# A gated dilated convolution on one core: one store for the last group, and first rows turned by products instead of transposes

## The chip, the cores and the metric

The kernel runs on 1 core of one Trainium2 chip. The metric is device time in microseconds (us) of one execution; the kernel before took 285.28 us (median of three runs). The engines are named as the profile names them: PE is TensorE (PEld its weight loads), DVE is VectorE, ACT is ScalarE, POOL is GpSimd, SP is SyncE; SPq and ACTq are the queues on which SP and ACT issue transfers.

## What is computed

The input x is 2 x 16000 x 256 in bf16, w is 3 x 256 x 512, w_o is 256 x 256.

```
xp = jnp.pad(x, ((0, 0), (pad, 0), (0, 0)))        # pad = 4, dilation 2
h = jnp.einsum('btc,cd->btd', xp[:, pad:pad + T, :], w[0])
for i in range(1, K):                               # K = 3
    off = pad - i * dil
    h = h + jnp.einsum('btc,cd->btd', xp[:, off:off + T, :], w[i])
f, g = h[..., :D], h[..., D:]
z = jnp.tanh(f) * _sigmoid(g)
return z @ w_o
```

Each output row needs its own row of x and those two and four rows before it.

## The kernel before

**Layout.** Four successive rows of x make one "r"; T / 4 = 4000 of them per batch are cut into groups of at most 256 (`groups`, built at lines 60 to 73). The first group of batch 0 has 160, the last two of batch 1 have 128 each. A tile `xt` holds a chunk of x turned, with channels on the partitions: `xt[:, j, ct, r]`, j being the row within the four. Rows j = 0, 1 are the x half, j = 2, 3 the y half; `views` (line 157) gives current and previous r of both as xc, yc, xp, yp.

**Steady work.** Groups 1 and on compute two rows per bank from sums and differences: DVE and POOL prepare `m`, `p` and `d` (lines 163 to 191), PE runs eight 128x512 products per step k (`products`, line 193, one step per group and block of 128 output channels), ACT copies bank b (`copy_m2`, line 234), DVE adds and subtracts in PSUM (`combine`, line 241), ACT applies tanh and sigmoid (`activate`, line 249), DVE multiplies (`gate`, line 266), and PE multiplies by w_o (`out_mm`, line 289). `out_evict` (line 303) copies the result to an SBUF tile `osb` and SP stores it. The order of all instructions is written by hand (`tc.manual_schedule()`, loop at lines 398 to 439). A group of 160 leaves 32 rows over: these "odd rows" are gated into `zo` and stored by four transfers of 32 partitions each (lines 308 to 314).

**The start.** At line 112 DVE clears a 128x128 tile `warm`, and PE multiplies it by itself 30 times (`warm_up(N_WARM[0])`, line 126) while the first transfers run. SP loads the first 640 rows of x as they are into `xn` (line 119); ACT issues the weights of taps 2 and 0, SP those of tap 1. Later chunks of x come by transposing transfers (line 106), which are slower to land, so the first group is turned on PE: `turn(i)` (lines 140 to 155) transposes tile i of 80 r's with the identity, 2 halves of j by 4 transposes, into a bf16 PSUM tile. The half h = 0 (rows j = 0, 1) is copied to `xt` by DVE, the half h = 1 by ACT. `turn(0)` and `turn(1)` are followed by six more warm-up products (line 370). Then the first group goes by plain products (`direct`, line 214): for each tap in the order 2, 0, 1 and each of three output blocks k, two products into bank a and two into bank b, 128x320 each. For tap 2 bank a reads only the half j = 0, 1 and bank b only the half j = 2, 3. PE then runs on with the steady steps.

**The end.** `finish` (line 324) multiplies the last group (128 r's) by w_o into four PSUM tiles (lines 340 to 347). For jp = 1 and then 0, ACT copies one tile and DVE the other into a tile `osb_end` (lines 350 and 351), and SP stores it by a transfer of 128 KB (line 353): two transfers.

Of the kernel before, what the change touches and what calls it, by code (L numbers as in the profile page):

```python
# [13 lines left out]
def kernel(  # L14
# [19 lines left out]
    nc = tc.nc  # L34
    bf16 = mybir.dt.bfloat16
    f32 = mybir.dt.float32
    B, T, D = x.shape
    K, _, D2 = w.shape
    P = 128
    assert K == 3 and D % P == 0 and D2 == 2 * D and T % 64 == 0  # L40
    CT = D // P
    NT = D // P
    RH = 16
    RG = 256
    N_WARM = (30, 6)
    O_ORDER = (0, 2, 1, 3)
    TAPS = (2, 0, 1)
    FIRST = (160,)
# [12 lines left out]
    for b in range(B):  # L61
        r0 = 0
        rs = sizes(FIRST if b == 0 else (), LAST[min(b, 1)])
        cuts = [1, 1] if b == 0 else []
        i = 0
# [10 lines left out]
    consts = ctx.enter_context(tc.tile_pool(name="consts", bufs=1))  # L76
# [7 lines left out]
    osb_pool = ctx.enter_context(tc.tile_pool(name="osb", bufs=4))  # L84
    ps_a = ctx.enter_context(tc.tile_pool(name="ps_a", bufs=3, space=bass.MemoryType.PSUM))
    ps_b = ctx.enter_context(tc.tile_pool(name="ps_b", bufs=3, space=bass.MemoryType.PSUM))
    ps_o = ctx.enter_context(tc.tile_pool(name="ps_o", bufs=2, space=bass.MemoryType.PSUM))
    ctx.enter_context(tc.manual_schedule())

    def warm_up(n):  # L90
        wps = ps_a.tile([P, 2 * RG], f32, name="a")
        for _ in range(n):
            nc.tensor.matmul(wps[:, :P], lhsT=warm[:], rhs=warm[:], start=True, stop=True)  # L93

    xts = {}

    def load_chunk(c):
# [11 lines left out]
        )  # L109


    warm = consts.tile([P, P], bf16)
    nc.vector.memset(warm[:], 0.0)  # L113
    w_taps = [consts.tile([P, CT, D2], bf16, name=f"w{k}_sb") for k in range(K)]
    wo_sb = consts.tile([P, NT, D], bf16)
    nx, rx = len(TILES), TILES[0][1]
    xn = consts.tile([P, nx, 4, D], bf16, name="xn")
    w_in = [w[k].rearrange("(ct c) d -> c ct d", c=P) for k in range(K)]
    nc.sync.dma_start(
        out=xn[:rx], in_=x[0, 0:4 * nx * rx, :].rearrange("(i r j) c -> r i j c", i=nx, j=4)  # L120
# [3 lines left out]
    nc.scalar.preload_act_table(ACT.Sigmoid)  # L124
    nc.sync.dma_start(out=w_taps[TAPS[2]][:], in_=w_in[TAPS[2]])
    warm_up(N_WARM[0])
    ident = consts.tile([P, P], bf16)
    make_identity(nc, ident[:])
# [8 lines left out]
    wp_sb = consts.tile([P, CT, D2], bf16)  # L137
    wm_sb = consts.tile([P, CT, D2], bf16)

    def turn(i):  # L140
        r0, r = TILES[i]
        for h in range(2):
            pool, tag = ((ps_o, "o_ps"), (ps_b, "b"))[i]
            tp = pool.tile([P, 2, CT, P], bf16, name="tp", tag=tag)
            for j in range(2):
                for ct in range(CT):
                    nc.tensor.transpose(  # L147
                        out=tp[:, j, ct, :r], in_=xn[:r, i, 2 * h + j, ct * P:(ct + 1) * P],
                        identity=ident[:r, :r],
                    )  # L150
            dst = xts[0][:, 2 * h:2 * h + 2, :, RH + r0:RH + r0 + r]
            if h == 0:
                nc.vector.tensor_copy(out=dst, in_=tp[:, :, :, :r])
            else:
                nc.scalar.copy(out=dst, in_=tp[:, :, :, :r])

    def views(g):
        G = groups[g]
        xt, c, R = xts[G["chunk"]], RH + G["col"], G["R"]
        return (xt[:, 0:2, :, c - 1:c - 1 + R], xt[:, 2:4, :, c - 1:c - 1 + R],  # L160
                xt[:, 0:2, :, c:c + R], xt[:, 2:4, :, c:c + R])
# [49 lines left out]
                start=first and ct == 0, stop=ct == CT - 1, skip_group_check=True,  # L211
            )

    def direct(k, taps):

        g, oi = divmod(k, 4)
        G = groups[g]
        o = O_ORDER[oi]
        osl = slice(o * P, (o + 1) * P)
        R = G["R"]  # L220
        xp, yp, xc, yc = views(g)
        for tap in taps:
            if tap == TAPS[0]:
                G["a", oi] = ps_a.tile([P, 2 * RG], f32, name="a")
                G["b", oi] = ps_b.tile([P, 2 * RG], f32, name="b")
            for bank, mv in (("a", (xc, yp, xp)[tap]), ("b", (yc, xc, yp)[tap])):
                for ct in range(CT):
                    nc.tensor.matmul(  # L228
                        G[bank, oi][:, :2 * R], lhsT=w_taps[tap][:, ct, osl], rhs=mv[:, :, ct, :],
                        start=tap == TAPS[0] and ct == 0, stop=tap == TAPS[-1] and ct == CT - 1,  # L230
                        skip_group_check=True,
                    )
# [16 lines left out]
    def activate(k):  # L249
        g, oi = divmod(k, 4)  # L250
        G = groups[g]
        R = G["R"]
        o = O_ORDER[oi]
        if oi == 0:
            G["th"] = act_pool.tile([P, NT, 4, RG], bf16, name="th")
            G["sg"] = act_pool.tile([P, NT, 4, RG], bf16, name="sg")
            G["z"] = z_pool.tile([P, NT, 4, RG], bf16, name="zz")
        dst = G["th"][:, o] if o < NT else G["sg"][:, o - NT]
        for h, bank in ((1, "b"), (0, "a")):
            nc.scalar.activation(  # L260
                out=dst[:, 2 * h:2 * h + 2, :R],
                in_=G[bank, oi][:, :2 * R].rearrange("p (q r) -> p q r", q=2),
                func=ACT.Tanh if o < NT else ACT.Sigmoid, scale=1.0 if g == 0 else 0.5,
            )
# [38 lines left out]
    def out_evict(g, rb0, jp, on_dve):  # L303
        G = groups[g]
        o_ps = G["o", rb0, jp]
        copy = nc.vector.tensor_copy if on_dve else nc.scalar.copy
        t0 = 4 * (G["r0"] + rb0)
        if jp is None:
            osb = osb_pool.tile([P, D], bf16, name="osb_odd")
            copy(out=osb[:], in_=o_ps[:, 0, :])  # L310
            rows = out[G["b"], t0:t0 + P, :].rearrange("(r j) d -> j r d", j=4)
            for j in range(4):
                nc.sync.dma_start(out=rows[j], in_=osb[j * P // 4:(j + 1) * P // 4, :])
            return
        if jp == 0:
            G["osb", rb0] = osb_pool.tile([P, 4, D], bf16, name="osb")
        osb = G["osb", rb0]
        copy(out=osb[:, 2 * jp:2 * jp + 2, :], in_=o_ps[:])  # L318
        if jp == 1:
            nc.sync.dma_start(  # L320
                out=out[G["b"], t0:t0 + 4 * P, :].rearrange("(p j) d -> p j d", j=4), in_=osb[:]
            )

    def finish(left):

        g = NG - 1
        G = groups[g]
        R = G["R"]
        assert R <= P
        dt = NT - 1  # L330
        activate(4 * g + 3)
        for piece in left:
            out_evict(*piece, False)
        for jp in (1, 0):
            js = slice(2 * jp, 2 * jp + 2)
            nc.vector.tensor_tensor(
                out=G["z"][:, dt, js, :R], in0=G["th"][:, dt, js, :R], in1=G["sg"][:, dt, js, :R], op=ALU.mult
            )
        tiles = {}
        for d in range(NT):  # L340
            for j in (2, 3, 0, 1):
                if d == 0:
                    tiles[j] = (ps_a, ps_b)[j % 2].tile([P, 2 * RG], f32, name="ab"[j % 2])
                nc.tensor.matmul(  # L344
                    tiles[j][:R, :D], lhsT=G["z"][:, d, j, :R], rhs=wo_sb[:, d, :],
                    start=(d == 0), stop=(d == NT - 1),
                )
        for jp in (1, 0):
            osb = osb_pool.tile([P, 2, D], bf16, name="osb_end")
            nc.scalar.copy(out=osb[:R, 0, :], in_=tiles[2 * jp][:R, :D])  # L350
            nc.vector.tensor_copy(out=osb[:R, 1, :], in_=tiles[2 * jp + 1][:R, :D])  # L351
            t0 = 4 * G["r0"]
            nc.sync.dma_start(
                out=out[G["b"], t0:t0 + 4 * R, :].rearrange("(p j) d -> p j d", j=4)[:, 2 * jp:2 * jp + 2, :],
                in_=osb[:R],
            )

    def drain(g, k, behind=None):

# [5 lines left out]
    NG = len(groups)  # L365
    NB = 4 * NG
    todo, made = [], []
    turn(0)
    turn(1)
    warm_up(N_WARM[1])  # L370
    for tap in TAPS:
        for k in range(3):
            direct(k, (tap,))
    nc.scalar.mul(wd0_sb[:], w_taps[0][:], 2.0)
# [11 lines left out]
    pre_d(1, 3, nc.gpsimd, last)  # L386

    direct(3, TAPS[:-1])
    products(N_DIRECT, 2)
    products(N_DIRECT, 1)  # L390
    copy_m2(N_DIRECT)
    direct(3, TAPS[-1:])
    activate(3)
    combine(N_DIRECT)
# [3 lines left out]
    k = N_DIRECT + 1  # L398
    while k <= NB:
        g, oi = divmod(k, 4)  # L400
# [7 lines left out]
        if k < NB:  # L408
            for piece in made:
                out_evict(*piece, g == NG - 1 and oi in (0, 2))  # L410
            made = []
# [27 lines left out]
        k += 1  # L439
    assert not todo  # L440
    finish(made)


# [28 lines left out]
```

## Time and profile before

| | |
|---|---|
| runs of the kernel before | 285.22, 285.28, 287.12 us |
| the profiled execution | 285.58 us |
| its span, first to last instruction | 283.6 us |
| PE busy | 279.1 us (98% of the span) |
| ACT, DVE, POOL busy | 260.8, 240.7, 126.1 us |
| first warm-up product on PE | 0.99 us after the span's start |
| first weight product (line 228) | 6.03 us |
| last product on PE starts | 279.80 us |
| second store of `osb_end` issued | 280.73 us |

How to read it: the span is what the profiler sees between the first and the last instruction; the execution's own time is 2.0 us more. A row of the timeline gives the start, the length, the engine, the line, the operation with the tile written and the tile read, a count, and in brackets how long the engine was idle before it and what ended that. PE's records overlap, since products are pipelined: the time between the starts of two says how fast they go, not the length of one.

### The profile page before, as it was taken

To read this page: it belongs to the slowest core of one execution; us is meant where nothing else is said; L and a number is where in the kernel's file an instruction comes from. 1 tells how busy PE (TensorE), PEld (TensorE's weight loads), DVE (VectorE), ACT (ScalarE), POOL (GpSimd) and SP (SyncE) were. 2 spreads that over 40 slices of the span, in tenths; PEclk is the share of its full clock that TensorE was granted. 3 is DMA by queue.
4 is the path that set the end of the run, shared out by engine and by line. 5 is a ranking of instruction groups with operands and counts; after the bars stand their busy time and mean duration, and the time that the engine had idled before them with its cause. 6 is when DMAs were issued, how large, how long until landed. Compare 5 with 4: busy or idle time off the path is not lost.

```text
span 283.6 us, 4830 instructions
## 1 busy us (share of the span) xinstructions
PE 279.1 (98%) x1624; PEld 158.2 (56%) x1624; DVE 240.7 (85%) x404; ACT 260.8 (92%) x521; POOL 126.1 (44%) x133
## 2 busy tenths in 40 slices
PE   8999999999999999999999999999999999999994
PEld 7645555555555555555555555555555555555783
DVE  1899888888888888888888888888888888888884
ACT  3689999999999999999999999999999999999995
POOL 1145454455445544544544454455445444543430
PEclk9999999999999999999999999999999999999999
DMA  8971891470925618163282823719146061311213
GB/s 213 196 153 46 194 221 42 124 179 37 226 76 88 178 61 201 74 156 110 77 189 76 184 79 103 190 48 226 47 120 177 37 162 74 82 74 72 80 74 120
DMA packets 76055, 34.50 MB, mean 122 GB/s; under 512 B 66528, under 2 KB 68064, under 8 KB 76032
## 3 DMA queue, kind: packets, MB, share of 16 engines
q1 hardware_dynamic: 75216, 33.56, 44.8%
q10 hardware_dynamic: 816, 0.66, 0.8%
q8 instruction: 12, 0.20, 0.3%
q14 instruction: 11, 0.09, 0.1%
HBM read 1.25 MB, written 16.38 MB: 62 GB/s over the span
## 4 chain that ended last, share of the span: by engine, by line
PE 98%; DVE 0%; DVEq 0%; issue 0%
PE a L209 37%; PE b L209 37%; PE o_ps L299 19%; PE a L93 1%; PE a L228 1%; PE b L228 1%; PE tp L147 0%; PE a L344 0%; DVE osb_end L351 0%; PE b L344 0%; DVEq L467 0%; DVE warm L113 0%
## 5 line engine op out<-in xcount | busy, mean ns | idle before, releaser
L184 POOL TENSOR_TENSOR dd<-xt 128x512 bf16<-128x512 bf16 (+2 forms) x125 | 125.2, 1002 | 147.7 <-DVE zz L278 64.6
L246 DVE TENSOR_TENSOR b<-a,ss 128x512 f32<-128x512 f32 (+2 forms) x128 | 86.5, 676 | 33.6 <-ACT ss L239 32.3
L247 DVE TENSOR_TENSOR a<-a,ss 128x512 f32<-128x512 f32 (+2 forms) x128 | 85.3, 667 | 0.0
L239 ACT COPY ss<-b 128x512 f32<-128x512 f32 (+2 forms) x128 | 72.8, 569 | 12.3 <-PE b L209 0.8
L209 PEld LDWEIGHTS <-wd_sb 128*128 128x128 bf16 x512 | 50.0, 98 | 56.2 <-issue 0.7
L209 PE MATMUL a<-dd,wd_sb 128*128 128x512 bf16 (+2 forms) x256 | 73.8, 370 | 0.0
L209 PE MATMUL b<-mm,wm_sb 128*128 128x512 bf16 (+2 forms) x256 | 73.8, 370 | 0.0
L209 PE MATMUL a<-pp,wp_sb 128*128 128x512 bf16 (+2 forms) x256 | 73.8, 370 | 0.0
L209 PE MATMUL b<-dd,wd_sb 128*128 128x512 bf16 (+2 forms) x256 | 73.8, 370 | 0.0
L299 PE MATMUL o_ps<-wo_sb,zz 128*128 128x256 bf16 x488 | 73.2, 273 | 0.0
L318 ACT CAST osb<-o_ps 128x512 bf16<-128x512 f32 x121 | 71.8, 593 | 0.0
L299 PEld LDWEIGHTS <-zz 128*128 128x128 bf16 x488 | 47.7, 98 | 29.6
L278 DVE TENSOR_TENSOR zz<-th,sg 128x1024 bf16<-128x1024 bf16 (+1 forms) x65 | 42.4, 653 | 0.0
L260 ACT ACTIVATE th<-b 128x512 bf16<-128x512 f32 (+2 forms) x66 | 39.3, 595 | 2.2 <-PE b L228 1.8
L209 PEld LDWEIGHTS <-wp_sb 128*128 128x128 bf16 x256 | 25.0, 98 | 27.9
L260 ACT ACTIVATE sg<-b 128x512 bf16<-128x512 f32 (+2 forms) x66 | 39.2, 594 | 0.7 <-PE b L228 0.4
L260 ACT ACTIVATE th<-a 128x512 bf16<-128x512 f32 (+2 forms) x66 | 39.3, 596 | 0.0
L260 ACT ACTIVATE sg<-a 128x512 bf16<-128x512 f32 (+2 forms) x66 | 39.2, 595 | 0.0
L209 PEld LDWEIGHTS <-wm_sb 128*128 128x128 bf16 x256 | 25.0, 98 | 3.7
L167 DVE TENSOR_TENSOR mm<-xt 128x1024 bf16<-128x1024 bf16 (+2 forms) x32 | 21.2, 663 | 0.0
L173 DVE TENSOR_TENSOR pp<-xt 128x1024 bf16<-128x1024 bf16 (+2 forms) x32 | 21.2, 663 | 0.0
L228 PEld LDWEIGHTS <-w_sb 128*128 128x128 bf16 x48 | 4.8, 100 | 2.1
(35 smaller groups left out, 40.0 us busy)
## 6 DMA issues: line engine op xcount, KB each, us to landing
out_dram<-osb SPq DMA_DIRECT2D x61, 256.0 KB, 2.1
w_sb<-in_w_dram ACTq DMA_DIRECT2D x2, 256.0 KB, 4.6
xn<-in_x_dram SPq DMA_DIRECT2D x1, 320.0 KB, 3.6
xt<-in_x_dram SPq DMA_TRANSPOSE x17, 6.5
w_sb<-in_w_dram SPq DMA_DIRECT2D x1, 256.0 KB, 4.5
out_dram<-osb_end SPq DMA_DIRECT2D x2, 128.0 KB, 1.9
wo_sb<-in_w_o_dram ACTq DMA_DIRECT2D x1, 128.0 KB, 3.5
out_dram<-osb_odd SPq DMA_DIRECT2D x8, 16.0 KB, 1.5
```

The lines of the kernel that those rows point to most:

```text
L167: return nc.vector.tensor_tensor(out=G["m"][:, :, :, :G["R"]], in0=xc, in1=yp, op=ALU.subtract)
L173: return nc.vector.tensor_tensor(out=G["p"][:, :, :, :G["R"]], in0=xc, in1=yp, op=ALU.add)
L184: ins = eng.tensor_tensor(out=G["d"][:, j, :, :R], in0=a[:, q], in1=s[:, q], op=ALU.subtract)
L209: nc.tensor.matmul(G[bank, oi][:, :N], lhsT=wmat[:, ct, osl], rhs=mv(ct), start=first and ct == 0, stop=ct == CT - 1, skip_group_check=True,)
L228: nc.tensor.matmul(G[bank, oi][:, :2 * R], lhsT=w_taps[tap][:, ct, osl], rhs=mv[:, :, ct, :], start=tap == TAPS[0] and ct == 0, stop=tap = ...
L239: nc.scalar.copy(out=G["ss", oi][:, :N], in_=G["b", oi][:, :N])
L246: nc.vector.tensor_tensor(out=pb[:, :N], in0=pa[:, :N], in1=ss[:, :N], op=ALU.subtract)
L247: nc.vector.tensor_tensor(out=pa[:, :N], in0=pa[:, :N], in1=ss[:, :N], op=ALU.add)
L260: nc.scalar.activation(out=dst[:, 2 * h:2 * h + 2, :R], in_=G[bank, oi][:, :2 * R].rearrange("p (q r) -> p q r", q=2), func=ACT.Tanh if o ...
L278: return nc.vector.tensor_tensor(out=G["z"][:, dt, :, :full], in0=G["th"][:, dt, :, :full], in1=G["sg"][:, dt, :, :full], op=ALU.mult)
L299: nc.tensor.matmul(o_ps[:, q, :], lhsT=lhsT, rhs=wo_sb[:, dt, :], start=(dt == 0), stop=(dt == NT - 1),)
L318: copy(out=osb[:, 2 * jp:2 * jp + 2, :], in_=o_ps[:])
```

## The change

Five edits: three at the start, one at the end, one in the odd rows:

- the warm-up multiplies a one-element-per-partition constant 1.0, which the program's preamble writes anyway, read as a 128x128 operand by repeating it; the tile `warm` and DVE's memset go;
- the first rows are turned by ordinary products with the identity into an f32 PSUM tile instead of transposes into a bf16 one, with the loop turned over: half h = 0 of both tiles first, then half h = 1 of both. The half h = 0 still is DVE's to copy, h = 1 ACT's. Three warm-up products follow instead of six;
- in the first group, tap 2 is done for bank a of all three output blocks and then for bank b; taps 0 and 1 as before;
- the last group's four copies go into one `osb` tile of the pool that the other groups use (four buffers), stored by one transfer of 256 KB;
- the odd rows are stored by one transfer instead of four.

```
-    N_WARM = (30, 6)
+    N_WARM = (30, 3)
...
-            nc.tensor.matmul(wps[:, :P], lhsT=warm[:], rhs=warm[:], start=True, stop=True)
+            nc.tensor.matmul(wps[:, :P], lhsT=warm, rhs=warm, start=True, stop=True)
...
-    warm = consts.tile([P, P], bf16)
-    nc.vector.memset(warm[:], 0.0)
+    warm = nc.const_aps.tensor(1.0, (P, P), bf16)
...
-    def turn(i):
+    def turn(i, h):
         r0, r = TILES[i]
-        for h in range(2):
-            pool, tag = ((ps_o, "o_ps"), (ps_b, "b"))[i]
-            tp = pool.tile([P, 2, CT, P], bf16, name="tp", tag=tag)
-            for j in range(2):
-                for ct in range(CT):
-                    nc.tensor.transpose(
-                        out=tp[:, j, ct, :r], in_=xn[:r, i, 2 * h + j, ct * P:(ct + 1) * P],
-                        identity=ident[:r, :r],
-                    )
+        pool, tag = ((ps_o, "o_ps"), (ps_b, "b"))[h]
+        tp = pool.tile([P, 2, CT, r], f32, name="tp", tag=tag)
+        for j in range(2):
+            for ct in range(CT):
+                nc.tensor.matmul(
+                    tp[:, j, ct, :], lhsT=xn[:r, i, 2 * h + j, ct * P:(ct + 1) * P], rhs=ident[:r, :r],
+                    start=True, stop=True,
+                )
...
-    def direct(k, taps):
+    def direct(k, taps, banks="ab"):
...
-            for j in range(4):
-                nc.sync.dma_start(out=rows[j], in_=osb[j * P // 4:(j + 1) * P // 4, :])
+            nc.sync.dma_start(out=rows, in_=osb[:])
...
+        osb = osb_pool.tile([P, 4, D], bf16, name="osb")
         for jp in (1, 0):
-            osb = osb_pool.tile([P, 2, D], bf16, name="osb_end")
-            nc.scalar.copy(out=osb[:R, 0, :], in_=tiles[2 * jp][:R, :D])
-            nc.vector.tensor_copy(out=osb[:R, 1, :], in_=tiles[2 * jp + 1][:R, :D])
-            t0 = 4 * G["r0"]
-            nc.sync.dma_start(
-                out=out[G["b"], t0:t0 + 4 * R, :].rearrange("(p j) d -> p j d", j=4)[:, 2 * jp:2 * jp + 2, :],
-                in_=osb[:R],
-            )
+            nc.scalar.copy(out=osb[:R, 2 * jp, :], in_=tiles[2 * jp][:R, :D])
+            nc.vector.tensor_copy(out=osb[:R, 2 * jp + 1, :], in_=tiles[2 * jp + 1][:R, :D])
+        t0 = 4 * G["r0"]
+        nc.sync.dma_start(out=out[G["b"], t0:t0 + 4 * R, :].rearrange("(p j) d -> p j d", j=4), in_=osb[:R])
...
-    turn(0)
-    turn(1)
+    for h in range(2):
+        for i in range(nx):
+            turn(i, h)
     warm_up(N_WARM[1])
-    for tap in TAPS:
+    for bank in "ab":
+        for k in range(3):
+            direct(k, TAPS[:1], bank)
+    for tap in TAPS[1:]:
         for k in range(3):
             direct(k, (tap,))
```

More of the change, by code (lines that the diff above doesn't have):

```diff
@@ L138 @@
     wm_sb = consts.tile([P, CT, D2], bf16)
-    def turn(i):
+    def turn(i, h):
         r0, r = TILES[i]
-        for h in range(2):
-            pool, tag = ((ps_o, "o_ps"), (ps_b, "b"))[i]
-            tp = pool.tile([P, 2, CT, P], bf16, name="tp", tag=tag)
-            for j in range(2):
-                for ct in range(CT):
-                    nc.tensor.transpose(
-                        out=tp[:, j, ct, :r], in_=xn[:r, i, 2 * h + j, ct * P:(ct + 1) * P],
-                        identity=ident[:r, :r],
-                    )
[L151 to L155, printed above, removed]
+        pool, tag = ((ps_o, "o_ps"), (ps_b, "b"))[h]
[6 more added lines that the diff above has]
+                )
+        dst = xts[0][:, 2 * h:2 * h + 2, :, RH + r0:RH + r0 + r]
+        if h == 0:
+            nc.vector.tensor_copy(out=dst, in_=tp[:])
+        else:
+            nc.scalar.copy(out=dst, in_=tp[:])
     def views(g):
@@ L222, in direct @@
         for tap in taps:
[L223 to L226, printed above, removed]
+            for bank in banks:
+                mv = ((xc, yp, xp) if bank == "a" else (yc, xc, yp))[tap]
+                if tap == TAPS[0]:
+                    G[bank, oi] = (ps_a if bank == "a" else ps_b).tile([P, 2 * RG], f32, name=bank)
                 for ct in range(CT):
```

## The prediction

> **What bounds the kernel now.** I read the page first (busy shares and the chain), then the timeline of the first 8 us and of the last 5, then the groups by shape for durations, then the DMA view.
>
> ```profile
> span 283.6 us, 4830 instructions
> ...
> PE 279.1 (98%) x1624; PEld 158.2 (56%) x1624; DVE 240.7 (85%) x404; ACT 260.8 (92%) x521; POOL 126.1 (44%) x133
> ...
> PE 98%; DVE 0%; DVEq 0%; issue 0%
> ```
>
> PE is the bound from end to end. It starts at 0.99 and its last product ends at 280.07 (279.80 + 0.27), a stretch of 279.08 against 279.1 busy: no gap that counts. So only two places can move the time: what PE does before its steady work, and what follows its last product. The change touches just these, besides the odd rows in the middle.
>
> The start:
>
> ```profile
> 0.82 0.11 DVE L113 MEMSET warm<- 128x64 uint32 x1 [0.82 <-PEq L456]
> 0.98 3.12 PEld L93 LDWEIGHTS <-warm 128*128 128x128 bf16 x30 [0.98 <-DVE warm L113]
> 0.99 3.38 PE L93 MATMUL a<-warm 128*128 128x128 bf16 x30 [0.99 <-DVE warm L113]
> ...
> 4.34 1.06 PEld L147 LDWEIGHTS <-xn 80*128 80x128 bf16 x16 [0.24 <-DMA xn<-in_x_dram]
> 4.35 1.25 PE L147 MATMUL tp<-ident,xn 80*128 80x80 bf16 x16
> 4.83 0.32 DVE L153 COPY xt<-tp 128x320 bf16<-128x320 bf16 x1 [3.90 <-PE tp L147]
> 5.10 0.96 ACT L155 COPY xt<-tp 128x320 bf16<-128x320 bf16 x2 [2.06 <-PE tp L147]
> ...
> 5.37 0.32 DVE L153 COPY xt<-tp 128x320 bf16<-128x320 bf16 x1 [0.21 <-PE tp L147]
> 5.39 0.84 PE L93 MATMUL a<-warm 128*128 128x128 bf16 x6
> 5.92 6.15 PEld L228 LDWEIGHTS <-w_sb 128*128 128x128 bf16 x44
> 6.03 0.64 PE L228 MATMUL a<-xt,w_sb 128*128 128x320 bf16 x2
> ...
> 6.50 0.44 PE L228 MATMUL b<-xt,w_sb 128*128 128x320 bf16 x2
> 6.78 0.44 PE L228 MATMUL a<-xt,w_sb 128*128 128x320 bf16 x2
> ```
>
> See two things. The turning of the first rows waits for the load of xn (4.34), not for the warm-up. And PE runs at half speed up to about 6.4: the warm-up products follow each other by 0.107 for 128 columns (six from 5.39 fill 0.64), the 16 transposes by 0.067 for 80, both 0.83 ns a column; the first two weight products take 0.47 from 6.03 to 6.50, the next pair 0.28, which is 0.43 ns a column. The page's clock row shows full speed throughout; the spacing says otherwise, and the trace's first record of a full clock stands at 6.43.
>
> The end:
>
> ```profile
> 279.67 0.69 ACT L350 CAST osb_end<-a 128x256 bf16<-128x256 f32 x2
> 279.78 0.76 DVE L351 CAST osb_end<-b 128x256 bf16<-128x256 f32 x2 [0.17 <-PE b L344]
> 279.80 0.35 SPq L320 DMA_DIRECT2D out_dram<-osb  x1
> ...
> 280.27 0.85 SPq L353 DMA_DIRECT2D out_dram<-osb_end  x2
> ```
>
> The last copy is done at 280.54; SP was busy issuing the first store, so the second is issued at 280.73 and lands 1.86 later, at 282.58. The span ends 1.0 after that.
>
> The sum is made against the profiled execution, 285.58 (span 283.6 and 2.0 around it). It is 0.30 over the median of 285.28; differences are carried to the median.
>
> **The change part by part.**
>
> *Warm-up from the constant.* PE waited 0.98 for DVE's memset (0.82 + 0.11). The other engines' first instructions stand at 0.73 to 0.82, so PE starts about 0.2 earlier, at 0.78. Directly worth nothing: the 30 products end 0.2 earlier and PE then waits longer for xn, 0.44 instead of 0.24. DVE loses a memset where it had nothing else. The constant is written by POOL by 0.41, before the engines are released, so no wait is added. A weight load that reads one column 128 times isn't in the trace; the nearest rows are L93's own loads and L147's, which keep the pace of their products. Bounds: nothing, or loads no longer hidden (the last rival). I take nothing, by the nearer row.
>
> *Products instead of transposes, order turned.* 16 matrix instructions of 80 columns either way, 0.83 ns a column in both kinds of instruction, so 16 x 0.067 again, from 4.34. What changes is the copies. The source is f32, and DVE has these rows:
>
> ```profile
> L247 DVE TENSOR_TENSOR a<-a,ss 128x320 f32<-128x320 f32 x4 | 2.0, 489 | 0.0
> ...
> L153 DVE COPY xt<-tp 128x320 bf16<-128x320 bf16 x2 | 0.6, 324 | 4.1 <-PE tp L147 4.1
> ...
> L310 DVE CAST osb_odd<-o_ps 128x256 bf16<-128x256 f32 x1 | 0.4, 418 | 0.0
> ```
>
> A copy of 320 columns from f32 lies between 0.32 (bf16 today) and 0.49 (the f32 add); from the 256-column f32 copy at 0.418 it is 0.48, so I take 0.49. DVE's two copies now come first: the first starts at 4.83 as before, the second waits for it and runs 5.32 to 5.81 (before: 5.37 to 5.69). ACT's two, for the other half, come later: after the 12th product (5.37) and then behind each other, 0.43 each, to about 6.23 (before 6.06).
>
> *Three warm-up products fewer.* 3 x 0.107 = 0.32 off PE: it is free at about 5.73 instead of 6.03. The first weight product then waits for DVE's copy at 5.81 + 0.05 (memset to weight load: 0.93 to 0.98) = 5.86; everything of PE stands behind it. Its weights landed at 4.84. Bank A first is what lets it go without ACT's half: six products of bank A cover at least 0.8 (6 x 0.137), so bank B comes after 6.7 and ACT's 6.23 is hidden by 0.4. Without that order PE would wait for 6.23 after two products.
>
> *Sum of the start.* After a wait a product of 80 columns ended 0.25 after its weight load started (L147, 4.34 to 4.59); with 240 columns more at 0.83 ns, 0.45. So the first weight product ends at 6.31 instead of 6.50, 0.19 earlier. But that is work at half speed, up to 6.43: 0.19 of it is worth 0.10 once the clock is up. With DVE's copy at 0.32 the warm-up's end at 5.73 decides and it is worth 0.15. I take 0.10. It carries to the end only if the suppliers are early: the tightest are the sums and differences for step 4, m ready at 10.76 for a product at 12.24, the last d at 13.50 for 14.95. More than 1 us of slack, so it carries.
>
> *Odd rows by one transfer.* Middle: four issues on SP (25.33 to 27.08) become one of about 0.4, so the next transposing load, issued at 27.18, is issued some 1.3 earlier. Nobody on PE waits for it: no gap. Slowed by stores it would have to lose all of 1.3 to land later than now. End: four issues from 276.67 to 278.40 become one; SP's next issue is at 279.80 and waits for ACT. Worth 0, covered by 1.4 of idle SP. If one strided transfer landed 1 us later (1.5 now), at about 279.5, it would still be done 3 before the last.
>
> *One store for the last group.* SP waits for the last copy, 280.54, and issues at 280.61 (0.06 after, as the first store did), 0.12 earlier than the second store now. A wait is added in front of the first copies (a used `osb` buffer must have been stored); that store was issued at 270.48 and landed by 272.5, 7 us before. For the landing:
>
> ```profile
> out_dram<-osb SPq DMA_DIRECT2D x61, 256.0 KB, 2.1
> ...
> out_dram<-osb_end SPq DMA_DIRECT2D x2, 128.0 KB, 1.9
> ```
>
> By the 256 KB row it lands at 280.61 + 2.06 = 282.67, 0.09 later than now. By the rate it doesn't: the store before lands at 281.86 and each 128 KB follows by 0.36, so both halves are in by 282.58, as now. Behind it SP waits for the transfers one after another, 0.06 each, one fewer now. So between +0.1 and -0.15; I take -0.05.
>
> Sum: -0.10 - 0.05 = -0.15; 285.28 becomes 285.1.
>
> **The rivals.**
>
> *The clock comes earlier.* Everything above leaves full speed at 6.43. The trace has one grant and can't tell what sets it; PE had been at work for 5.4 us by then. If it comes before the turn, the first weight product still waits for DVE's copies (5.86, or up to 0.1 sooner as four products take half the time), and ends 0.32 later (0.45 less 320 columns at 0.40 ns): 6.08 to 6.18. Now the first two end at 6.50 and 6.67, which at full speed's spacing of 0.137 is as if the first ended at 6.53. That gains 0.35 to 0.45, taken as 0.40. With the tail's 0.05: 284.85. For it: PE starts 0.2 earlier, and no transposes stand between. Against it: 0.2 of 5.4 is little, and PE has more idle time. [...]
>
> *The clock comes later (slower than before).* The warm-up ends 0.2 sooner and PE then idles 0.44 + 0.13 (before the first weight product) instead of 0.24. If idle time in the stretch before 6.43 is what the clock is held back for, the grant slips. At half speed every us of slip costs 0.5. The place is the gap at 4.0 to 4.34; it decides from the point where 0.57 of idle is too much and 0.24 is not. The slip isn't in the trace; rows near it: the clock was taken back at 282.91, 2.84 after PE's last product, and given 5.44 after its first. So 1.4 to 2.7 lost. One of the three runs shown was 1.84 above the others, which lies within that: 285.28 - 0.15 + 1.8 = 286.9. [...]
>
> *The constant's weight loads are slow.* 30 products must be done in 3.56 (0.78 to 4.34), 0.119 each; they take 0.107. If load and product went one after the other, 0.107 + 0.148 (L93's mean load), the warm-up ends at 8.4 and the turn is 4.1 late, partly at full speed: up to 289. Against it: nothing in the operands asks for it, and the loads ran beside products in every row.
>
> **How the numbers follow.** The forecast 0.52 (own range 284.9 to 285.5: the tail's bounds and DVE's copy); clock earlier 0.28 (284.85); clock later 0.14 (286.9); slow loads 0.03 (289); something not listed 0.03. The range takes the first two with their bounds and the scatter of the runs shown: 284.4 to 286.0, leaving out the last three, 0.20. One per cent (2.85 us, about what a measurement of this kernel can tell) is more than any case but slow loads: faster by over 1% 0.01, within 0.96, slower 0.03.
>
> **What would show it.** In the profile of the changed kernel: warm-up's first product at 0.75 to 0.85; turning still at 4.34; DVE's copies 0.49 each, the second ending at 5.8; the first weight product ending at 6.3; no PE gap before bank B; the spacing of weight products falling from 0.27 to 0.14 at about 6.4 (earlier: the first rival; at 8 or later: the second); one last store issued 0.06 after the last copy, landing within 2.1. I am wrong if PE shows gaps in the middle, if the copies from f32 take over 0.6, or if the turn starts after 4.4.

## The result and the profile after

The changed kernel took 286.91 us (median of 22 runs, 285.03 to 287.46), the kernel before 285.25 (22 runs, 284.79 to 287.55). The ratio of the means is 1.0034, with an interval of 1.0018 to 1.005: a little slower, where 285.1 in 284.4 to 286.0 had been forecast. The gap between the medians is large because the runs of both kernels lie in two groups with nothing between 286.1 and 286.7: of the changed kernel 8 runs at 285.0 to 285.6 and 14 at 286.8 to 287.5, of the kernel before 19 at 284.8 to 286.0 and 3 at 287.1 to 287.6. The change moved runs from the one group to the other. Below, runs over 286.4 are called late. (Some expectations speak of 13 late runs of 22; it is 14.)

The profiled execution of the changed kernel, 287.08 with a span of 285.1, is a late one. Its page:

```profile
span 285.1 us, 4817 instructions
...
PE 280.6 (98%) x1621; PEld 158.4 (56%) x1621; DVE 240.9 (84%) x403; ACT 260.7 (91%) x521; POOL 126.1 (44%) x133
...
PE 97%; DMA 1%; DVE 0%; DVEq 0%; issue 0%
```

PE has three products fewer and is busy 1.5 longer, as much as the span grew. So no new wait in the middle: products ran more slowly somewhere. The timeline of its start says where:

```profile
0.78 3.36 PE L93 MATMUL a<-const-bfloat16-1.0 128*128 128x128 bf16 x30 [0.78 <-PEq L455]
...
4.36 1.25 PE L146 MATMUL tp<-ident,xn 80*128 80x80 bf16 x16 [0.23 <-DMA xn<-in_x_dram]
4.85 0.89 DVE L152 CAST xt<-tp 128x320 bf16<-128x320 f32 x2 [4.85 <-PE tp L146]
...
5.38 0.75 ACT L154 CAST xt<-tp 128x320 bf16<-128x320 f32 x2 [2.34 <-PE tp L146]
5.41 0.52 PE L93 MATMUL a<-const-bfloat16-1.0 128*128 128x128 bf16 x3
...
5.88 1.76 PE L227 MATMUL a<-xt,w_sb 128*128 128x320 bf16 x6
...
7.44 1.80 PE L227 MATMUL b<-xt,w_sb 128*128 128x320 bf16 x6
...
9.04 0.74 PE L227 MATMUL a<-xt,w_sb 128*128 128x320 bf16 x2
9.57 0.54 PE L227 MATMUL b<-xt,w_sb 128*128 128x320 bf16 x2
9.95 0.43 PE L227 MATMUL a<-xt,w_sb 128*128 128x320 bf16 x2
```

Down to 5.9 the forecast steps are there: warm-up at 0.78, turn at 4.36, DVE's copies (0.49 and 0.48 by the trace) done at 5.74, the first weight product ending at 6.31. But six weight products of 320 columns fill 1.56 (5.88 to 7.44) and the next six 1.60 (7.44 to 9.04), 0.27 each, which is half speed; two take 0.38 from 9.57 to 9.95, and from there on 0.27. The full clock comes at 9.79 by the trace's clock record, where it came at 6.43 before. Being 3.35 later at half speed costs 1.68; less the 0.1 gained ahead of it and 0.02 in the tail, 1.56, against 1.52 by which the span grew.

The end of the changed kernel:

```profile
281.21 0.69 ACT L348 CAST osb<-a 128x256 bf16<-128x256 f32 x2
...
281.33 0.76 DVE L349 CAST osb<-b 128x256 bf16<-128x256 f32 x2 [0.17 <-PE b L342]
...
282.14 0.33 SPq L351 DMA_DIRECT2D out_dram<-osb  x1
```

The copies are done at 282.08, the store is issued 0.06 later and lands 2.01 after that. From the end of PE's last product to the span's end it is 3.53, before 3.55.

### The profile page after: what moved, and what is told of

Same layout as the page of the kernel before. It is cut to its first block, busy times and chain, and to the rows that moved or that the text cites. A ratio compares the mean times of both kernels' runs of the same rounds, so it can differ in the third digit from the quotient of the medians.

```text
span 285.1 us, 4817 instructions
## 1 busy us (share of the span) xinstructions
PE 280.6 (98%) x1621; PEld 158.4 (56%) x1621; DVE 240.9 (84%) x403; ACT 260.7 (91%) x521; POOL 126.1 (44%) x133
## 4 chain that ended last, share of the span: by engine, by line
PE 97%; DMA 1%; DVE 0%; DVEq 0%; issue 0%
PE a L208 37%; PE b L208 37%; PE o_ps L298 19%; PE a L227 2%; PE b L227 1%; DMA xn<-in_x_dram 1%; PE tp L146 0%; PE a L342 0%; DVE osb L349 0%; PE b L342 0%; DVEq L466 0%; PE a L93 0%
```

## When the full clock came

The trace of each profiled execution has the moments at which the full clock was given and taken back. In 13 of the 20 it was held for 276.48 us, those of the kernel before and of the changed kernel among them, in 7 for 279.89. The moment of the grant, counted from the span's start, differs from execution to execution: 3.48, 4.02, 4.31, 5.25, 5.72, 6.43, 6.69 among the early runs, 8.86 and 9.79 in the two late ones (e5 and the changed kernel). What the grant goes by isn't in the traces: they hold the moment and no reason.

| kernel | warm-up products before and behind the turn | full clock in the profiled run, us | late runs |
|---|---|---|---|
| before | 30, 6 | 6.43 | 7 of 144 |
| changed | 30, 3 | 9.79 | 14 of 22 |
| second pause filled (e2) | 30, 6 | 3.48 | 0 of 12 |
| start edits only (e10) | 30, 3 | 3.64 | 2 of 12 |
| 26 warm-up products (e3) | 26, 6 | 4.31 | 7 of 12 |
| stores only (e16) | 30, 6 | 6.69 | 11 of 24 (e7, e9) |
| warm-up of 80 rows (e5) | 30, 6 | 8.86 | 6 of 6 |

The moment in one profiled run doesn't tell the kernels apart: in e3, with 7 of 12 runs late, the clock came earlier than in the kernel before. The changed kernel and e2 have the same 30 products ahead of the turn, from 0.78 and 0.77 on, and the clock came at 9.79 in the one and 3.48 in the other. So the experiments go by how many runs are late.

## The experiments

The theory behind the first four (A), a supposition: the grant needs PE at work for most of a fixed stretch, and the change has put more pause into it. The runs can show what the pauses do; such a stretch and its length they don't show. Rivals: B, the constant isn't counted; C, products instead of transposes, or the order, make it late.

**e1: pause before the turn filled.** The changed kernel with

```
-    N_WARM = (30, 3)
+    N_WARM = (33, 3)
```

> The changed kernel with 33 instead of 30 warm-up products ahead of the turn; the three more end about 0.1 before xn lands, so PE's pause before the turn shrinks from 0.41 to 0.09 us and nothing is delayed. Theory A (the clock is granted only when PE was at work for nearly all of some fixed stretch before the grant; 0.41 plus the 0.12 before the first weight product is too much pause): the grant comes at about 6.4 as in the kernel before, the late runs (286.8 to 287.5, 13 of 22 of the changed kernel) all but vanish, median 285.0 to 285.4. Rival B (the repeated constant doesn't count as work for the clock): as the changed kernel, median 286.9. Rival C (products in place of transposes, or bank A first, make it late): median 286.9.

Measured 285.13 (12 runs, one late); the kernel before beside it 285.20 (35 runs, two late); ratio 0.9993 (0.9973 to 1.0013). The changed kernel itself was not run again beside the experiments; its 14 late runs of 22 are those above. That is what A forecast; B and C fall: constant, products and order are all in it. PE's part of its trace:

```profile
0.77 3.68 PE L93 MATMUL a<-const-bfloat16-1.0 128*128 128x128 bf16 x33 [0.77 <-PEq L455]
4.33 1.15 PE L146 MATMUL tp<-ident,xn 80*128 80x80 bf16 x16
...
5.85 0.98 PE L227 MATMUL a<-xt,w_sb 128*128 128x320 bf16 x6 [0.20 <-DVE xt L152]
```

The turn follows the warm-up without a pause. Six weight products take 0.82 here (the next six start at 6.67), full speed from the first.

**e2: second pause filled.** The changed kernel with six warm-up products behind the turn again.

```
-    N_WARM = (30, 3)
+    N_WARM = (30, 6)
```

> The changed kernel with six warm-up products behind the turn instead of three: the pause of 0.12 before the first weight product goes, the pause of 0.41 before the turn stays; the first weight product comes 0.2 later, still at half speed, which costs 0.1. Theory A with a limit between 0.41 (some early runs of the changed kernel must have had that much in their stretch) and 0.53: no late runs, median 285.2 to 285.5. If the limit lies below 0.41, late runs stay, median about 287. Rivals B and C: median about 287.

Measured 285.15 (284.85 to 285.53, 12 runs, none late); ratio 0.9995 (0.9981 to 1.0009). As A forecast. So it is enough to fill either of the two pauses: with one before the turn and none behind it no run of 12 is late.

**e3: the pause put into the kernel before.**

```
-    N_WARM = (30, 6)
+    N_WARM = (26, 6)
```

> The kernel before with 26 instead of 30 warm-up products ahead of the turn, nothing else: PE pauses 0.59 before the turn instead of 0.16. Theory A: nearly all runs late, spread over 286.0 to 287.5, median about 286.8; the grant in the profile after 7.8. Rivals B and C: no constant, no products, old order, so as the kernel before, median 285.2.

Measured 286.86 (12 runs, 7 late); ratio 1.0034 (1.001 to 1.0058), the changed kernel's loss made with nothing of the change but a pause. A expected nearly all late; five weren't. The profiled run is one of these five: the clock was given at 4.31, while PE still waited for xn (the turn began at 4.61). Why it came in time in these five is not shown.

**e4: the constant alone, in the kernel before.**

```
-            nc.tensor.matmul(wps[:, :P], lhsT=warm[:], rhs=warm[:], start=True, stop=True)
+            nc.tensor.matmul(wps[:, :P], lhsT=warm, rhs=warm, start=True, stop=True)
...
-    warm = consts.tile([P, P], bf16)
-    nc.vector.memset(warm[:], 0.0)
+    warm = nc.const_aps.tensor(1.0, (P, P), bf16)
```

> The kernel before with the warm-up taken from the repeated constant, nothing else: PE starts 0.2 earlier and pauses 0.41 before the turn; there is no second pause. Theory A with a limit over 0.41: as the kernel before, few late runs, median 285.2. Rival B: most runs late, median 286.5 or more. Rival C: median 285.2.

Measured 285.18 (12 runs, one late); ratio 0.9996 (0.9979 to 1.0013). B falls again: with the constant, ending earlier, and six products behind the turn one run of 12 is late; of the kernel before beside it two of 35 are.

**e5 and e6: rows or columns.** The turn's products use 80 of the 128 rows and have 80 columns; those of the warm-up have 128 of both. The kernel before with a warm-up of 80 rows (e5), and with one of 80 columns in the same time (e6):

```
e5
-            nc.tensor.matmul(wps[:, :P], lhsT=warm[:], rhs=warm[:], start=True, stop=True)
+            nc.tensor.matmul(wps[:, :P], lhsT=warm[:80, :], rhs=warm[:80, :], start=True, stop=True)
e6
-    N_WARM = (30, 6)
+    N_WARM = (48, 10)
...
-            nc.tensor.matmul(wps[:, :P], lhsT=warm[:], rhs=warm[:], start=True, stop=True)
+            nc.tensor.matmul(wps[:, :80], lhsT=warm[:], rhs=warm[:, :80], start=True, stop=True)
```

> The kernel before with a warm-up that multiplies only 80 of the 128 rows, same count, same columns, same spacing, so that PE's pauses are unchanged. [...] Theory A1 (work counts by the rows in use): the stretch before a grant needs about a microsecond of full products, so the grant comes at 7.2 to 10.6, nearly all runs at 285.7 to 287.3, median 286.5. Rival A2 (only pauses count): no change from the kernel before, median 285.2.

> The kernel before with warm-up products of 80 columns and all 128 rows, 48 and 10 of them instead of 30 and 6, so that they fill the same time. The turn's products differ from the warm-up in rows and in columns. Theory A1 (rows count): as the kernel before, median 285.2. Rival A3 (short products, or many weight loads, count for less): most runs late, median 286.5 or so. Rival A2: 285.2.

e5 measured 286.92 (286.56 to 288.11, all six runs late; ratio 1.0051, 1.0035 to 1.0067), e6 285.29 (11 runs, none late; ratio 0.9984, 0.9969 to 0.9999). With 80 rows in the warm-up every run is late, with 80 columns none. That is what A1 forecast; the microsecond of full products that it asks for is a guess, and no run shows such a figure. PE in e5:

```profile
0.99 3.38 PE L93 MATMUL a<-warm 80*128 80x128 bf16 x30 [0.99 <-DVE warm L113]
4.80 1.25 PE L147 MATMUL tp<-ident,xn 80*128 80x80 bf16 x16 [0.43 <-DMA xn<-in_x_dram]
5.85 0.84 PE L93 MATMUL a<-warm 80*128 80x128 bf16 x6
6.48 0.74 PE L228 MATMUL a<-xt,w_sb 128*128 128x320 bf16 x2
...
8.62 0.56 PE L228 MATMUL a<-xt,w_sb 128*128 128x320 bf16 x2
9.02 0.44 PE L228 MATMUL b<-xt,w_sb 128*128 128x320 bf16 x2
```

The warm-up has the pace it always had (30 products fill 3.38, as in the kernel before), but the full clock comes at 8.86, 2.38 after the start of the first 128-row product (6.48). See also that xn landed 0.45 later than in the kernel before: the turn's start varies by itself, from 4.13 to 4.80 in the profiled runs, and with it the pause.

**e10, e11, e12: the start's edits taken apart.** e10 is the changed kernel with both stores of the kernel before, e11 the kernel before with products in the turn, e12 the changed kernel with the warm-up tile cleared by VectorE again.

```
e11
-            tp = pool.tile([P, 2, CT, P], bf16, name="tp", tag=tag)
+            tp = pool.tile([P, 2, CT, r], f32, name="tp", tag=tag)
...
-                    nc.tensor.transpose(
-                        out=tp[:, j, ct, :r], in_=xn[:r, i, 2 * h + j, ct * P:(ct + 1) * P],
-                        identity=ident[:r, :r],
-                    )
+                    nc.tensor.matmul(
+                        tp[:, j, ct, :], lhsT=xn[:r, i, 2 * h + j, ct * P:(ct + 1) * P], rhs=ident[:r, :r],
+                        start=True, stop=True,
+                    )
e12
-    warm = nc.const_aps.tensor(1.0, (P, P), bf16)
+    warm = consts.tile([P, P], bf16)
+    nc.vector.memset(warm[:], 0.0)
...
-            nc.tensor.matmul(wps[:, :P], lhsT=warm, rhs=warm, start=True, stop=True)
+            nc.tensor.matmul(wps[:, :P], lhsT=warm[:], rhs=warm[:], start=True, stop=True)
```

> The changed kernel with the stores of the kernel before: only the edits of the start. Theory A1: as late as the changed kernel, about 7 of 12 runs at 286.8 to 287.5. Rival D: fewer late, at most 3 of 12.

> The kernel before with the turn by products into an f32 tile instead of transposes, in the old order and with the old warm-up. Theory A1: the turn counts by its 80 rows in either kind, so the same as the kernel before, at most 2 of 12 late, median 285.2 (0.0 to 0.1 more for the copies from f32). Rival E (transposes don't count as work and products do): no late run and the early ones earlier, median 284.9 or less. Rival C (products in place of transposes make it late): most late.

> The changed kernel with the warm-up tile cleared by VectorE again, so that PE starts at 0.98 and the 30 products end 0.2 later; all other edits stay. The pause before the turn is 0.16 to 0.2 instead of 0.41, the one before the first weight product stays. Theory A1: hardly any late run, median 285.2. Rival C: half of the runs late, median 286 or more.

e11 measured 285.23 (11 runs, none late; ratio 0.9997, 0.998 to 1.0014): the kind of instruction makes no difference to the time. e12 measured 285.38 (12 runs, one late; ratio 1.0014, 1.0002 to 1.0026): with the old, later warm-up the late runs go, the other edits staying; so among the edits of the start it is the warm-up that ends too soon. e10 measured 285.26 (12 runs, 2 late; ratio 1.0016, 1.0 to 1.0033), where A expected about seven late. The changed kernel and e10 have the same start and together 16 late runs of 34, so a part of what parts them may be chance, and a part the stores, which come next.

**e7, e9, e13, e14: the stores alone, in the kernel before.** Their edits are those of the change, at lines 312 to 313 and 348 to 356 of the kernel before; e7 and e9 have both, e13 the odd rows', e14 the last group's.

> The kernel before with the two store edits of the change alone (last group by one transfer, odd rows by one). Forecast of the tail: from PE's last product to the span's end 3.55 now; the changed kernel showed 3.53, so 3.45 to 3.60 here, and the median 285.1 to 285.3 with as few late runs as the kernel before. Rival: the store's edits are part of the loss, median 285.5 or more.

> The kernel before with the two store edits alone, a second time. The first time 5 of 12 runs were late (287.1 to 287.8) where the kernel before has some 7 in 100 late, though the stores come 270 us after the clock's grant. Theory A1 (only what PE does before the grant matters): the five were chance, at most 2 of 12 late here, median 285.2 to 285.5. Rival D (the store edits make the start late too, by way of what the transfers leave behind for the next start): again 4 to 6 of 12.

> The kernel before with the odd rows' single transfer alone. Rival D, told apart by halves: if this edit makes the late runs, 5 or 6 of 12 late; if the last group's store does, at most 2 of 12, median 285.2. Theory A1 (only PE's work before the grant counts): at most 2 of 12 in both.

> The kernel before with the last group's single store alone. Rival D: 5 or 6 of 12 late if this edit makes the late runs; else at most 2 of 12, median 285.2. Theory A1: at most 2 of 12 in both.

e7 measured 285.49 with 5 of 12 late (ratio 1.0022, 1.0 to 1.0045), e9 286.42 with 6 of 12 (1.0038, 1.0017 to 1.0058), e13 285.44 with 4 of 12 (1.002, 0.9998 to 1.0042), e14 285.55 with none of 12 (1.001, 1.0 to 1.0019). In the five sets of runs of the kernel before 7 of 144 were late. So what D expected came for the odd rows' edit: in the kernel before it goes with 15 late runs of 36. That it acts by what its transfers leave behind is not shown. It isn't enough with every start either: e1, e2, e8 and e12 hold it and have 4 late runs of 48. Theory A doesn't say why it should matter. In e7, e9 and e13 that transfer is first issued at 24.75, 25.42 and 24.43, after the grant, and the profiled runs, all three early, show nothing odd: the turn began at 4.38, 4.40 and 4.22 (before: 4.35), the clock came at 4.75, 6.55 and 4.14. The tail of e7 is 3.54, that of the kernel before 3.55, as forecast for it. e15 to e18 are four single executions of the kernel of e7, profiled to catch the trace of a late run:

> The kernel before with both store edits, one look for the trace of a late run (about one in two). [...]

> [...]

> As the two looks before (both early): the kernel before with both store edits, for the trace of a late run, about two in five. [...] Rival G: the grant came in time and PE stalled some 1.8 later on.

> As the look before, a fourth. [...]

They measured 285.32, 285.67, 285.13 and 285.56, none late, so there is no trace of a late run of that kernel. The granted clock recorded with every run speaks against G. It falls short of 1 only by the time after the full clock is taken back: the kernel before shows 0.999, half of the 0.7 us of its span behind 282.91, though its first 6.43 us were at half speed. In the changed kernel's profiled run, with its late grant, the clock is taken back at 286.27, behind the span's end, and the share is 1.0. It is 1.0 in all 14 late runs of the changed kernel and in all 15 of e7, e9 and e13, but in only 5 of the 21 early runs of these three. A grant in time with a stall of PE later on would leave the share as spread as in the early runs. So their late runs look like late grants too; why that edit brings them, and whether A holds for them, stays open.

**e8: pause filled, copies shared by tile.** The changed kernel with

```
-    N_WARM = (30, 3)
+    N_WARM = (33, 1)
...
-        if h == 0:
+        if i == 0:
             nc.vector.tensor_copy(out=dst, in_=tp[:])
```

> The changed kernel with 33 warm-up products ahead of the turn and one behind it, and with the copies shared the other way: DVE copies both halves of the first tile, ACT both of the second. Bank A's half is then ready at about 5.54 instead of 5.75, since the two copies run side by side. Theory A: hardly any late run, and 0.1 to 0.2 less than with the gap alone filled (285.13): median 285.0. Rival: bank B, whose last copy ends about 6.1, or the clock decides and the copies' 0.2 us is worth nothing: 285.15.

Measured 285.39 (12 runs, two late); beside it the kernel before 285.46; ratio 1.0002 (0.9987 to 1.0018). No gain can be seen. Its trace shows one thing that can limit an earlier start:

```profile
16.20 1.04 POOL L183 TENSOR_TENSOR dd<-xt 128x512 bf16<-128x512 bf16 x1 [2.78 <-DMA xt<-in_x_dram]
16.29 1.49 DVE L166 TENSOR_TENSOR mm<-xt 128x1024 bf16<-128x1024 bf16 x1
...
18.45 0.59 PE L208 MATMUL b<-dd,wd_sb 128*128 128x512 bf16 x2 [0.56 <-DVE b L245]
```

The third piece of x landed at 16.06 (12.85 to 16.06 in the profiled runs). DVE stood in its queue waiting for it, its sum for the next step came late, and PE lost 0.72 there by the ends of its products. No version tried beats the kernel before beyond the interval; e1 and e2 come level with it.

## Why the prediction was wrong, point by point

- **The steps that failed** are two terms that were put at nothing. The first is the earlier warm-up: "Directly worth nothing: the 30 products end 0.2 earlier and PE then waits longer for xn, 0.44 instead of 0.24". The pause was sized about rightly (0.41 by the ends of the products), but its price was not nothing: in the profiled run, which has this pause and the second one, the full clock comes at 9.79 instead of 6.43, and 3.35 more at half speed cost 1.68. The pause alone makes 7 of 12 runs of the kernel before late (e3); with it filled (e1), or the later start given back (e12), 1 of 12 is late. The second term is the odd rows' transfer, "Worth 0": with the old stores given back, the same start is late in 2 of 12 (e10), and that edit alone goes with 15 late runs of 36. How much of the 14 of 22 belongs to which is open.
- **A premise of the sum**, "Everything above leaves full speed at 6.43", took the moment of one run for that of the kernel. In the profiled early runs, whatever the kernel, the grant lies anywhere from 3.48 to 6.69.
- **The rival that came true** is the second, at its price: 286.9 forecast for it, 286.91 measured, with a chance of 0.14. That they agree to 0.01 is luck: the price came from the one late run of three, the late runs of the changed kernel have a median of 287.24, and the median of all falls among them only because more than half were late. The rival's place was right: with either pause filled, 1 and 0 of 12 runs are late (e1, e2). Idle time alone, its measure, doesn't cover what the runs show: e5 kept the pace and the number of the warm-up's products, on 80 rows, and all six runs were late.
- **The three warm-up products taken out** were counted as 0.32 off PE. Given back (e2), the late runs are gone, none of 12. In the changed start it takes both pauses, the one before the turn (0.41) and the one that these three products had covered (0.12), to make them; a sum that prices each step by itself can't see that.
- **The rival of an earlier clock** counted it for the change that no transposes stand between. No row of before shows that they hold the clock back, and e11, products in the turn of the kernel before, shows no gain from that: 285.23, the kernel before beside it 285.24, ratio 0.9997 (0.998 to 1.0014). Nor does PE's earlier start alone (e4): 285.18 against 285.20, ratio 0.9996 (0.9979 to 1.0013).
- **The sum of the start**, 0.10, held where the clock is late: first weight product ending at 6.31. Where the clock comes early it has the other sign, which the prediction put at a gain of 0.40. From the turn's start to the first weight product it is 1.11 in e14, whose start is the old one, and 1.40 in e2, whose start is the new one but for the three warm-up products (1.39 in e10, which lacks them), all with the clock given by 4.02. PE there waits for DVE's two copies from f32, 0.49 each, one behind the other:

```profile
4.36 0.75 PE L147 MATMUL tp<-ident,xn 80*128 80x80 bf16 x16
4.94 0.50 PE L93 MATMUL a<-warm 128*128 128x128 bf16 x6
5.47 0.44 PE L228 MATMUL a<-xt,w_sb 128*128 128x320 bf16 x2
```

```profile
4.13 0.75 PE L146 MATMUL tp<-ident,xn 80*128 80x80 bf16 x16 [0.24 <-DMA xn<-in_x_dram]
4.72 0.52 PE L93 MATMUL a<-const-bfloat16-1.0 128*128 128x128 bf16 x6
5.53 0.98 PE L227 MATMUL a<-xt,w_sb 128*128 128x320 bf16 x6 [0.29 <-DVE xt L152]
```

  The first fence is e14, the second e2; the bracket at 5.53 is the wait. So the early runs of the changed kernel gain nothing either: their median is 285.35, that of the early runs before 285.22, against a forecast of -0.15.
- **The tail** held: store 0.06 after the last copy, landing 2.01 later (2.06 forecast), 0.02 gained of the 0.05 taken. Over the profiled kernels the time from PE's last product to the span's end is 3.55 to 3.58 with two stores and 3.52 to 3.54 with one, but for e13 (two stores, 3.40) and e14 (one, 3.70), which stay unexplained.
- **The odd rows** were costed at nothing, with SP's idle time as cover. PE shows no wait for them, but e7, e9 and e13 say the edit isn't free. The working had no place where it could cost anything, and the runs don't show one.
- **The slow weight loads** of the repeated constant can be ruled out: its 30 loads fill 3.12, as the old ones did.
- **The range** left out the case that came. The three runs shown held one at 287.12. I read it as the size of a slip and not as its frequency. Of all runs of the kernel before 7 of 144 were late, so one in three overstates it; but a value that had been seen belonged in the range.

## What to carry to other kernels

A warm-up is worth what it does for the clock. Here, moving it earlier by 0.2 us without making it longer widened the pause in front of the data's arrival from 0.16 to 0.41, and a pause there alone put 7 of 12 runs of the kernel before some 1.9 us behind the others (e3, medians 287.12 and 285.18): more than all that the change was to save, 0.15. Cover the wait for the first data to its end, look at the rows that small products use and not only at their time (e5: 80 of 128 rows, six of six runs late), and look at the distribution of runs, not only at one profile: where a time comes in two groups, a change can shift runs between them while the rows of a profile look better. And an edit that no row of the profile prices can still go with such a shift, as the odd rows' transfer did here.

## What the runs showed of the hardware that was not expected

- The time that PE was at work is not all that counted here: a warm-up of 80-row products at an unchanged pace (30 fill 3.38 either way) made all six runs late (e5, 286.56 to 288.11), one of 80-column products in the same time none of 11 (e6, 284.74 to 285.90).
- The full clock outlasted the work. In the run of e3 it stayed until 284.20, 4.64 after PE's last product at 279.56; in that of the kernel before until 282.91, 2.84 after the last product's end.
- The load of xn, the same transfer issued at the same 0.74 in every kernel, landed between 4.30 and 4.75 where its landing is recorded; the turn that waits for it began between 4.13 and 4.80.
